# Sink-window attention, Fourier mixing and FFN on one core: the second FFN product of token groups 2 to 5 as seven Strassen products

## The chip, the cores and the metric

The kernel runs on one core of a Trainium2 chip, in one launch. Time is device time in microseconds (us), from one execution to the next some tenths of a per cent apart: three runs of the kernel before gave 766.65, 764.19 and 766.62, a median of 766.62. The engines are TensorE (PE in the profile, its weight loads PEld), VectorE (DVE), ScalarE (ACT), GpSimd (POOL) and SyncE (SP), which here issues the DMAs. Each engine takes its own instructions in order and waits for the others at semaphores.

## The reference

Attention with 4 sink tokens and a window of 128, over 4 batches, 8 heads, 768 tokens and 64 features a head, gives `x` of 4 x 768 x 512. Then, all in float32:

```python
X = np.fft.fft(np.fft.fft(x, axis=1), axis=2)
u = x + np.real(X).astype(np.float32)
mu = np.mean(u, axis=-1, keepdims=True)
var = np.mean((u - mu) ** 2, axis=-1, keepdims=True)
un = (u - mu) / np.sqrt(var + 1e-06)
ch = np.maximum(un @ w_ch1, 0.0) @ w_ch2
return (u + ch).astype(np.float32)
```

`w_ch1` is 512 x 2048 and `w_ch2` is 2048 x 512. The change lies in the last product, `relu(...) @ w_ch2`.

## The kernel before

**Precision.** Every large product is made of three: a matrix is split into a high part, rounded by a write in the type fp32r, and the low remainder (x minus its high part), and high x high, high x low and low x high are accumulated in PSUM. A split costs an ACT operation (the high part) and a DVE or POOL subtraction (the low part). `split` (L1148) does it for the hidden values, with the ReLU in it: ACT at L1149, DVE at L1150.

**Groups.** The 24 blocks of 128 tokens (order of batches 0, 2, 1, 3) are cut into six groups of four blocks, 512 tokens each. Attention and the Fourier mixing run until the page's 212th microsecond or so; group 0's FFN overlaps their end, together with the conversion of the weights. From there on groups 1 to 5 run one after the other, from about 338 us to 757 us of the span, in one loop written out by hand under `tc.manual_schedule()`: on each engine the instructions stand in the order of the program text. `u` of batches 0 and 2 lives in SBUF (`U`), that of batches 1 and 3 in DRAM (`u_dram`), and `reload` brings a group's `u` into places that are free again.

**The first product** (x times w1) already goes by Strassen's scheme in Winograd's form, with seven products in place of eight. `w_dram` holds, for each of 8 pairs of feature blocks, four quarters' worth of sums and quarters of w1, split, as made by `combine_w1` (L630 to L652) during group 0: POOL makes four sums of 256 columns (`tq`), ACT the high parts, POOL the low parts (`to`, L647). A group takes NIT = 4 rounds (`it`), each with seven products k = 0 to 6 (`product`, L1322), and every product is 12 matmuls of 256 columns. Its weights, 512 KB (a tile), are two DMAs of 256 KB from `w_dram` into one of eight places; `load(n + 8)` (L1297) stands behind product n, so eight tiles are under way or waiting. The other operand is `state["x"]`: the seven sums of x, split. PSUM banks A, B and C take the products in the order ABCABCB, and DVE adds them up: L1384, L1394, L1395, L1400, L1403 into `tmp`.

**The second product** is the plain one. `halves` splits a result into one of four places of `hring`, and `unit` (L1350) multiplies it by w2, which stays in SBUF as `Wt[f, 1]` (high and low): 12 matmuls of 512 columns for a unit, 16 units in a group, put between the products of the first. They accumulate over the whole group in four banks `o0` to `o3`, and `finish` (L1162, L1163) adds `u` on DVE and stores the block.

**The next group's preparation.** `prepare(g + 1)` is a generator, and the products call it a step at a time: layer norm statistics, reciprocal roots, the normalized block (L541), and its transpose in 32 x 32 squares by DVE (L1209, 64 instructions a group) into `xf`. In the last round `sums(g + 1, G)` makes the seven sums of x on POOL (L1230 to L1236) and `put` their splits (ACT L1240, POOL L1241).

Of the kernel before, what the change touches and what calls it, by code (L numbers as in the profile page):

```python
# [53 lines left out]
PREP_N = 3  # L54
NPR, NIT, NWS = NF // 2, NF // 4, 8
# [150 lines left out]
def kernel(  # L206
# [29 lines left out]
    w_dram = [dpool.tile([P, 7, 512], F32, name=f"wd{i}") for i in range(NPR)]  # L236

# [34 lines left out]
    def run(general):  # L272
        tag = "g" if general else ""
        with ExitStack() as p1:
# [889 lines left out]

            def u_of(b, blk):

                return U[b if b in U else b - 1][:, blk, :]

            def reload(g):

                left = {}
                for b, blk in groups[g]:
                    if b in U:
                        left.setdefault(b, []).append(blk)
                for b, l in left.items():
                    nc.sync.dma_start(U[b][:, l[0]:l[-1] + 1, :], u_dram[b + 1][:, l[0]:l[-1] + 1, :])
# [6 lines left out]
            def prepare(g):  # L1183
# [10 lines left out]
                for i, u in enumerate(us):  # L1194
# [9 lines left out]
                    else:  # L1204
                        un = un_.pop((b, blk))
                        for a in range(4):
# [4 lines left out]
                            yield  # L1211
# [79 lines left out]
            n_all = (len(groups) - 1) * NIT * 7  # L1291

            def load(n):
                if n < n_all:
                    it, k = divmod(n % (NIT * 7), 7)
                    for j in range(2):
                        nc.sync.dma_start(f32(places[n % NWS][:, j]).rearrange("p s c -> p (s c)"), w_dram[2 * it + j][:, W_PLACE[k]])  # L1297
# [8 lines left out]
            with tc.manual_schedule():  # L1306
                wr = p1.enter_context(tc.tile_pool(name="wr" + tag, bufs=1, side="right"))
                tmp = npool.tile([P, 6, 512], F32, tag="ring", name="tmp", bufs=1)
# [3 lines left out]
                p1c, u2, u3, c22, c12, c21 = (tmp[:, i] for i in range(6))  # L1312

                def product(n, ps):
                    k = n % 7
# [38 lines left out]

                for n in range(LDB, NWS):
                    load(n)
                n = 0
                for g in range(1, len(groups)):
                    steps = prepare(g + 1) if g + 1 < len(groups) else iter(())
                    for it in range(NIT):  # L1360
                        put = lambda k: None
                        if it == NIT - 1 and g + 1 < len(groups):
                            for _ in steps:
                                pass
                            start, put = sums(g + 1, G)
                            start()

                        def step():
                            next(steps, None)

                        ps = {}
                        for k in range(7):
                            if BANK.index(BANK[k]) == k:
                                pool, t = {"B": banks[it % 2][:2]}.get(BANK[k], (state["h"], {"A": "h", "C": "cw"}.get(BANK[k])))
                                kw = dict(bufs=1) if BANK[k] == "B" else {}
                                ps[BANK[k]] = pool.tile([P, 512], F32, tag=t, name=f"p{BANK[k]}_{g}_{it}", **kw)
                            product(n, ps[BANK[k]])
                            n += 1
                            a, b, c = (ps.get(x) for x in "ABC")
                            put(k)  # L1380
                            if k == 0:
                                A.copy(p1c, a)
                            elif k == 1:
                                V.tensor_tensor(u2, b, p1c, op=ALU.add)  # L1384
                                unit()
                                step()
                            elif k == 3:
                                halves(g, it, 0, 0, a)
                                unit()
# [101 lines left out]
```

## Time and profile before

| what | value |
|---|---|
| runs shown | 766.65, 764.19, 766.62 us; median 766.62 |
| profiled execution | 766.28 us, its span 764.6 us |
| mean granted TensorE clock | 0.992 |
| busy: PE, DVE, ACT, POOL | 729.8, 528.8, 267.1, 279.1 us |
| chain that ended last, by engine | PE 72%, DVE 12%, POOL 5% |
| largest line of that chain | L1350, the second product, 29% |
| L1350, `o<-w,hring` | 780 matmuls of 512 columns |
| HBM read and written | 120.77 MB and 24.13 MB |

The page and the answers of the trace use the same line numbers as the code above. A row of a group view gives line, engine, operation, output and inputs, the shape, how often it occurs, the busy time, the mean in nanoseconds, and the idle time in front of it with what ended it. A row of the timeline begins with the start and the length in us. The mean of one matmul row is its way through the array and longer than the distance from one matmul to the next, so distances are read from starts.

### The profile page before, as it was taken

The page shows a single profiled execution, that of the slowest core. Times are in us where ns is not written, and L with a number is a line of the kernel's source. Part 1 is how long each engine was busy: PE and PEld are TensorE (multiplying, and loading weights), DVE is VectorE, ACT ScalarE, POOL GpSimd, SP SyncE. Part 2 cuts the span into 40 slices and gives each one's busy share as a digit, 9 for nine tenths or more (in the row PEclk, how much of TensorE's full clock was granted, in tenths as well). Part 3 has the DMA queues.
Part 4 walks back from the last instruction along what each step waited for, and adds up shares of the span by engine and source line. Part 5 has one row for each costly group of instructions (what it writes and reads, how often), then busy time and mean ns, then how long its engine had stood idle before and what let it go on. Part 6 is the DMA issues. An engine that isn't in the chain of part 4 may idle for free.

```text
span 764.6 us, 13878 instructions
## 1 busy us (share of the span) xinstructions
PE 729.8 (95%) x4899; PEld 622.5 (81%) x4899; DVE 528.8 (69%) x1411; ACT 267.1 (35%) x743; POOL 279.1 (37%) x387
## 2 busy tenths in 40 slices
PE   7999998989989989899999999999999999999995
PEld 5676876867878768678899889989899889889884
DVE  6878588888899988867774778467855777342223
ACT  4787666666624335421123111321122111311110
POOL 2467467577548788740034000510043002500000
PEclk9999999999999999999999999999999999999998
DMA  9764525532317798789555865567655655575501
GB/s 297 260 169 124 144 72 171 167 100 96 103 43 259 266 333 301 269 284 395 186 179 168 281 196 167 168 220 251 191 178 183 219 175 174 176 242 163 175 27 60
DMA packets 84447, 145.91 MB, mean 191 GB/s; under 512 B 7532, under 2 KB 32236, under 8 KB 82960
## 3 DMA queue, kind: packets, MB, share of 16 engines
q1 hardware_dynamic: 84080, 141.17, 56.9%
q0 software_dynamic: 288, 3.76, 1.2%
q8 instruction: 41, 0.67, 0.4%
q14 instruction: 38, 0.31, 0.1%
HBM read 120.77 MB, written 24.13 MB: 190 GB/s over the span
## 4 chain that ended last, share of the span: by engine, by line
PE 72%; DVE 12%; POOL 5%; issue 3%; ACT 2%; DMA 2%; SPq 1%; ACTq 0%; DVEq 0%; POOLq 0%
PE o L1350 29%; PE pB L1322 11%; PE pC L1322 7%; PE pA L1322 7%; PE xt L837 4%; PE s L742 4%; PE pt L799 2%; PE za L396 2%; PE h L659 2%; PE zb L396 1%; DVE sm L761 1%; PE o L1157 1%; DVE cw L602 1%; DVE cw L601 1%; DVE s L748 1%
## 5 line engine op out<-in xcount | busy, mean ns | idle before, releaser
L1350 PE MATMUL o<-w,hring 128*128 128x512 f32 x780 | 192.0, 392 | 0.0
L1350 PEld LDWEIGHTS o<-w,hring 128*128 128x128 f32 x780 | 142.5, 188 | 27.9
L1149 ACT ACTIVATE hring<-tmp 128x512 fp32r<-128x512 f32 x60 | 37.9, 632 | 174.9 <-DVE tmp L1395 84.7
L1230 POOL TENSOR_TENSOR s<-xf 128x512 f32<-128x512 f32 x4 | 5.2, 1295 | 241.1 <-DVE xf L1209 241.1
L1150 DVE SCALAR_TENSOR_TENSOR hring<-tmp,hring 128x512 fp32r<-128x512 f32 x60 | 51.8, 864 | 45.6 <-ACT hring L1149 45.6
L1209 DVE STREAM_TRANSPOSE xf<-un 32x128 f32<-32x128 f32 x256 | 77.4, 302 | 3.5
L767 ACT ACTIVATE sm<-sm,mx 128x132 f32<-128x132 f32 x192 | 76.0, 400 | 4.7 <-DVE mx L761 4.7
L1322 PE MATMUL pB<-x,w_b 128*128 128x256 f32 x456 | 59.4, 279 | 0.6 <-DMA w_b<-wd 0.6
L1322 PEld LDWEIGHTS pB<-x,w_b 128*128 128x128 f32 x456 | 56.6, 188 | 1.7 <-DVE stat L518 0.8
L659 PE MATMUL h<-un_slots,w_ring 128*128 128x512 f32 x192 | 50.6, 412 | 7.4 <-DVE h L1150 7.2
L742 PE MATMUL s<-ring,q 64*128 64x260 f32 x320 | 49.3, 412 | 7.8 <-DVE mx L761 3.5
L761 DVE CUSTOM_DVE_ANT_0 sm<-s,mask 128x132 f32<-128x132 f32 x192 | 48.5, 293 | 8.2 <-PE s L740 2.8
L1150 DVE SCALAR_TENSOR_TENSOR hring<-pA,hring 128x512 fp32r<-128x512 f32 x20 | 13.8, 692 | 56.4 <-ACT hring L1149 56.4
L659 PEld LDWEIGHTS h<-un_slots,w_ring 128*128 128x128 f32 x192 | 36.7, 198 | 17.6 <-DVE h L1150 7.0
L1149 ACT ACTIVATE hring<-pA 128x512 fp32r<-128x512 f32 x20 | 11.9, 596 | 99.8 <-PE pA L1322 99.8
L742 PEld LDWEIGHTS s<-ring,q 64*128 64x128 f32 x320 | 26.9, 185 | 20.4 <-issue 6.6
L1350 PE MATMUL o<-w_gh,hring 128*128 128x512 f32 x120 | 42.5, 395 | 0.0
L1157 PE MATMUL o<-w,h 128*128 128x512 f32 x156 | 39.1, 395 | 1.1 <-POOL w L627 0.5
L837 PE MATMUL xt<-ptl,ldv 128*64 128x128 f32 x384 | 39.3, 285 | 0.0
L1322 PEld LDWEIGHTS pC<-x,w_b 128*128 128x128 f32 x288 | 36.9, 188 | 2.0
L1322 PE MATMUL pA<-x,w_b 128*128 128x256 f32 x288 | 37.5, 279 | 0.2 <-DMA w_b<-wd 0.2
L1322 PE MATMUL pC<-x,w_b 128*128 128x256 f32 x288 | 37.4, 279 | 0.0
(216 smaller groups left out, 1528.7 us busy)
## 6 DMA issues: line engine op xcount, KB each, us to landing
w_b<-wd SPq DMA_DIRECT2D x172, 256.0 KB, 3.4
w_c<-wd SPq DMA_DIRECT2D x108, 256.0 KB, 3.4
raw<-in_moe_w_ch_dram SPq DMA_DIRECT2D x32, 512.0 KB, 4.8
wd<-to SPq DMA_DIRECT2D x8, 1024.0 KB, 5.1
ldv<-in_v_dram SPq DMA_DIRECT2D x28, 256.0 KB, 3.1
ring<-in_qk_dram SPq DMA_DIRECT2D x24, 264.0 KB, 4.5
wd<-w_ring SPq DMA_DIRECT2D x8, 768.0 KB, 3.9
out_dram<-u SPq DMA_DIRECT2D x24, 256.0 KB, 2.3
```

The lines of the kernel that those rows point to most:

```text
L396: T.matmul(ps[:, :NK], a, c, start=i == 0, stop=i == len(mm) - 1)
L659: T.matmul(ps[:, :tb], a[cc], x[:, :, cc, :], start=n == 0, stop=n == 3 * NCC - 1)
L742: T.matmul(ps[:, j, :P + W], st["q", g][rows, hp, :], keys(g, 2 * hp + j), start=True, stop=True)
L761: V.tensor_tensor_reduce(sm[:, h % 4], ps[:, j, P:P + W], mask[min(qi, 3)], -SCALE, 3.0e38, ALU.add, ALU.min, accum_out=mx[:, 0, h:h + 1])
L767: A.activation(sm[:, h % 4], sm[:, h % 4], AF.Exp, bias=mx[:, 0, h:h + 1], scale=-1.0, accum_out=mx[:, 1, h:h + 1])
L837: T.matmul(ps[D * j:D * j + D, p, :], st["v", kb(g) - i][:, h, :], a[:, h % 4, :], start=i == 0, stop=i == n - 1)
L1149: state["relu"] = A.activation(h[0], x, AF.Relu).ins
L1150: V.scalar_tensor_tensor(h[1], x, 0.0, f32(h[0]), op0=ALU.max, op1=ALU.subtract)
L1157: T.matmul(po[i], a[:, ts_], x, start=f == 0 and n == 0, stop=f == NF - 1 and n == 2)
L1209: V.transpose(place[32 * q:32 * q + 32, :, r], un[r].rearrange("p (c q j) -> p c q j", c=NCC, q=4)[:, :, q])
L1322: T.matmul(ps[:, 256 * j:256 * j + 256], w[:, j, a, cs], x[:, xs], start=BANK.index(BANK[k]) == k and j == c == m == 0, stop=j == c == 1 a ...
L1350: T.matmul(po[i], h[:, a, j, ts_], x, start=first and j == m == 0, stop=last and j == 1 and m == 2)
```

## The change

Group 1 keeps the old second product. In its first three rounds it also makes sums of w2's quarters; groups 2 to 5 then multiply by Strassen's scheme over all 2048 features at once. For these groups the first product comes first as a whole, 28 products, two rounds (index i) interleaved; then the second, 28 steps `s2`, as seven products k with four steps c each.

Making the sums, for each of the 8 pairs p, at fixed turns of group 1 (0 to 27 of 40): two DVE sums of 512 columns that put high and low of w2 together, four POOL sums of 256, two ACT copies and two POOL differences, and a store of 1 MB from SP's queue into `t_dram`.

```diff
+t_dram = [dpool.tile([P, 4, 512], F32, name=f"td{i}") for i in range(NPR)]
...
+def whole_w2(p):
+    for j in range(2):
+        w = Wt[2 * p + j, 1]
+        V.tensor_tensor(sums_r[0][:, j], f32(w[0]), f32(w[1]), op=ALU.add)
...
+def split_w2(p):
+    q, o = sums_q, sums_o
+    for j in (0, 2):
+        A.copy(o[:, j:j + 2, 0].bitcast(F32R), q[:, j:j + 2])
+        G.tensor_tensor(o[:, j:j + 2, 1].bitcast(F32R), q[:, j:j + 2], o[:, j:j + 2, 0], op=ALU.subtract)
...
+    t0 = 26 * p // NPR
+    for d, fn in ((0, whole_w2), (1, sums_w2), (4, split_w2), (5, store_w2)):
+        w2_at.setdefault(t0 + d, []).append((fn, p))
```

Three of the four sums (products k = 1, 2, 4) are loaded for every group, twelve tiles more in the same stream of eight places; the fourth is loaded once, in group 2's k = 0, over the quarters of w2 that it replaces (16 DMAs, 2 MB in all). The other four products use w2 as it stands in SBUF.

```diff
+stream = [(w_dram, it, W_PLACE[k]) for it in range(NIT) for k in range(7)]
+for g in range(2, len(groups)):
+    stream += [(w_dram, i, W_PLACE[k]) for it in range(0, NIT, 2) for k in range(7) for i in (it, it + 1)]
+    stream += [(t_dram, it, T_PLACE[k]) for k in (1, 2, 4) for it in range(NIT)]
```

In the first product's 28 steps DVE adds up the results as before, ACT applies the ReLU, and for each round POOL makes two of the sums of the hidden values:

```diff
+    V.tensor_tensor(t_[c], p, t_[c], op=ALU.add)
+    A.activation(t_[c], t_[c], AF.Relu)
+    G.tensor_tensor(X[3][c], t_[c], X[1][c], op=ALU.subtract)
+    G.tensor_tensor(t_[c], X[4][c], X[3][c], op=ALU.add)
+if t == 2 and 3 < g + 1 < len(groups):
+    reload(g + 1)
+if t in (14, 15, 24, 25):
+    split_h(c_ := (14, 15, 24, 25).index(t), 0, c_, V)
+for _ in range(CH1_PREP[g > 2][t]):
+    next(steps, None)
```

with `CH1_PREP = [[0] + [1, 2, 1] * 9, [0] * 6 + [1, 1, 2] * 7 + [1]]`; each preparation turn of groups 3 to 5 is now two transposes. In the second product each step is 12 matmuls of 256 columns; an operand is split four steps ahead of its use, by ACT and DVE, for k = 2 by ACT and POOL:

```diff
+def split_h(n, k, c, eng):
+    h = hring[:, n % 4]
+    hi, lo = (h[:, j].rearrange("p j t -> p (j t)") for j in range(2))
+    x = {0: X[1], 1: t_, 2: X[1], 3: X[2], 4: X[3], 5: X[2], 6: X[4]}[k][c]
+    A.copy(hi, x)
+    eng.tensor_tensor(lo, x, f32(hi), op=ALU.subtract)
...
+for s2 in range(7 * NIT):
+    k, c = divmod(s2, NIT)
...
+    product2(s2, k, c, n, p)
+    if k in (1, 2, 4):
+        load(n + NWS)
+        n += 1
+    if s2 + 4 < 7 * NIT:
+        k4 = (s2 + 4) // NIT
+        split_h(s2 + 4, k4, (s2 + 4) % NIT, G if k4 == 2 else V)
+    if k == 0:
+        G.tensor_tensor(X[1][c], X[1][c], t_[c], op=ALU.add)
+    if k == 3:
+        G.tensor_tensor(X[2][c], X[2][c], t_[c], op=ALU.subtract)
+    if c == NIT - 1:
+        for half, m in (((0, 1), (1, 0), (1, 1)), ((0, 1),), ((1, 1),), ((0, 0),), ((1, 1),), ((0, 1),), ((1, 0),))[k]:
+            add_u(g, half, m, p)
+        if k >= 5:
+            store_u(g, k - 5)
```

The results are added to `u` on DVE, nine additions of 512 columns a group, and stored in two halves behind k = 5 and k = 6. The rest of the preparation runs here, one turn a step, and behind it `sums_x(g + 1)`, which replaces `sums`: four POOL sums and seven splits (ACT and POOL), again one turn a step. In group 2 it begins at step 9, in groups 3 and 4 at step 16. `tmp` and other places in SBUF are handed out anew for `X`; the places for `u` of groups 3 to 5 change with them.

More of the change, by code (lines that the diff above doesn't have):

```diff
@@ L1311, in run, with product @@
                 hring = npool.tile([P, 4, 2, 2, 256], F32R, tag="un_slots", name="hring", bufs=1)
-                p1c, u2, u3, c22, c12, c21 = (tmp[:, i] for i in range(6))
-                def product(n, ps):
-                    k = n % 7
+                more = [wr.tile([P, 2, 512], F32, name="more")] if general else []
+                last_chunk = wr.tile([P, 512], F32, name="last_chunk")
+                p1c, u2, u3, c21 = (tmp[:, i] for i in range(4))
+                def product(n, k, ps):
                     w = places[n % NWS]
@@ L1357, in run @@
                 n = 0
[L1358 to L1389, printed above, removed]
-                                step()
-                                if it == 0:
-                                    reload(g - 1)
-                            elif k == 4:
-                                V.tensor_tensor(u3, b, p1c, op=ALU.add)
-                                V.tensor_tensor(c22, u3, c, op=ALU.add)
-                                halves(g, it, 1, 1, c22)
-                                unit()
-                                step()
-                            elif k == 5:
-                                V.tensor_tensor(c12, u2, c, op=ALU.add)
-                                halves(g, it, 1, 0, c12)
-                            elif k == 6:
-                                V.tensor_tensor(c21, b, p1c, op=ALU.add)
-                                halves(g, it, 0, 1, c21)
-                                unit()
-                            step()
@@ L1407, in run @@
                 while done[0] < len(units):
                     unit(1)
+                assert not w2_at, w2_at
+                x12 = npool.tile([P, 2, NIT, 512], F32, tag="ring", name="x12", bufs=1)
+                x3 = [npool.tile([P, 2, 512], F32, tag="tw", name=f"x3_{i}", bufs=1 if general else 2) for i in range(2 - len(more))]
+                x3 += more
+                X = {
+                    1: [x12[:, 0, c] for c in range(NIT)],
+                    2: [x12[:, 1, c] for c in range(NIT)],
+                    3: [x3[c // 2][:, c % 2] for c in range(NIT)],
+                    4: [npool.tile([P, 512], F32, tag="qs0", name=f"x4_{c}", bufs=QSB) for c in range(NIT - 1)] + [last_chunk],
+                }
```

204 lines of the change are left out of this document (191 added, 13 removed).

## The prediction

> **What bounds the kernel now.** I read the page for the engine shares, then busy time by stage, then the order of work on TensorE inside a group, then the rows where POOL and DVE meet. The profiled execution took 766.28 us, 0.34 below the median of the runs shown (766.62); all sums start from 766.3.
>
> ```profile
> span 764.6 us, 13878 instructions
> PE 729.8 (95%) x4899; PEld 622.5 (81%) x4899; DVE 528.8 (69%) x1411; ACT 267.1 (35%) x743; POOL 279.1 (37%) x387
> ```
>
> The next view gives busy time by stage. Groups 1 to 5 run from 338 to 757 us, some 83.7 us each. The first four rows are the four rounds (`it` 0 to 3) of group 1, the fifth is group 2, the last is group 5.
>
> ```profile
> 338.00:359.00 21.00, 20.19 (x140) 18.52 (x139) 15.15 (x43) 3.67 (x6) 0.00 (x0) 1.00 1.00 374
> 359.00:380.00 21.00, 21.00 (x135) 18.87 (x133) 15.50 (x41) 3.08 (x5) 0.00 (x0) 1.00 0.70 230
> 380.00:401.00 21.00, 21.00 (x134) 18.97 (x133) 15.74 (x36) 4.11 (x7) 6.31 (x5) 1.00 0.56 175
> 401.00:422.00 21.00, 21.00 (x135) 18.97 (x134) 8.64 (x12) 6.08 (x10) 8.64 (x7) 1.00 0.56 180
> 422.00:505.50 83.50, 83.50 (x530) 75.38 (x529) 56.07 (x131) 16.35 (x27) 14.93 (x11) 1.00 0.63 203
> 673.00:757.00 84.00, 83.85 (x518) 74.83 (x516) 28.10 (x42) 11.73 (x19) 0.00 (x0) 1.00 0.42 133
> ```
>
> Columns: length, then PE, PEld, DVE, ACT, POOL busy, the granted clock, the DMA share, GB/s. TensorE is busy without a gap: it alone bounds the changed stage, at the full clock. DVE has 56 us of 83.5, of which 28 are the preparation of the next group (group 5 prepares nothing and shows 28.10). POOL has 15.
>
> ```profile
> 500.67 1.58 PE L1322 MATMUL pA<-x,w_c 128*128 128x256 f32 x12
> 502.08 1.59 PE L1322 MATMUL pB<-x,w_c 128*128 128x256 f32 x12
> 503.51 2.93 PE L1350 MATMUL o<-w,hring 128*128 128x512 f32 x12
> 506.28 1.58 PE L1322 MATMUL pC<-x,w_c 128*128 128x256 f32 x12
> 507.69 1.57 PE L1322 MATMUL pA<-x,w_b 128*128 128x256 f32 x12
> 509.11 2.92 PE L1350 MATMUL o<-w,hring 128*128 128x512 f32 x12
> ```
>
> From start to start, twelve matmuls of 256 columns take 1.415 us (506.28 to 509.11, halved), twelve of 512 take 2.77. I call 1.415 us a step.
>
> **TensorE.** A group now has 28 steps and 16 units of 2.77: 39.6 + 44.3 = 83.9, as seen. The change replaces the 16 units by 28 steps in groups 2 to 5: 44.3 - 39.6 = 4.7 saved, **-18.8** for four. The rest asks what makes TensorE wait.
>
> **The hand-over to the second product.** Before, the two products alternate, so each result has steps to spare. Now product 2 of the second product (index k=2) needs `X[1]+t_`, and POOL alone makes it. Its queue at that place: `X[3]` and `t_` for the last two quarters (4), `X[1]` for all four (4), the first difference of `split_h` (1): nine operations of 512 before step 8 may start. The prices:
>
> ```profile
> 398.98 1.30 POOL L1241 TENSOR_TENSOR x<-xf,x 128x512 fp32r<-128x512 f32 x1 [0.76 <-ACT x L1240]
> 400.25 1.29 POOL L1241 TENSOR_TENSOR x<-s,x 128x512 fp32r<-128x512 f32 x1
> ```
> ```profile
> L1384 DVE TENSOR_TENSOR tmp<-pB,tmp 128x512 f32<-128x512 f32 x20 | 13.8, 692 | 19.9 <-PE pB L1322 18.6 <-ACT tmp L1382 1.1
> L1149 ACT ACTIVATE hring<-tmp 128x512 fp32r<-128x512 f32 x60 | 37.9, 632 | 174.9 <-DVE tmp L1395 84.7 <-DVE tmp L1400 53.9 <-DVE tmp L1403 35.8
> L1209 DVE STREAM_TRANSPOSE xf<-un 32x128 f32<-32x128 f32 x256 | 77.4, 302 | 3.5
> ```
>
> POOL starts one every 1.27 us. Product 26 ends one step before the second product starts, with a tail of 0.16 us (a row of twelve lasts 1.58, not 1.415), so its result is there at -1.25; DVE's sum (0.69) and ACT's ReLU (0.63) bring POOL's start to about 0.2. Nine times 1.27 is 11.4, so 11.6 against the 11.3 at which step 8 is due. That is late even with nothing in the way. Two things are in the way.
>
> ```profile
> 395.22 1.30 POOL L1231 TENSOR_TENSOR s<-s,xf 128x512 f32<-128x512 f32 x1
> 396.48 1.75 POOL L1232 TENSOR_TENSOR s<-xf 128x512 f32<-128x512 f32 x1
> ```
> ```profile
> 395.25 1.82 DVE L1150 SCALAR_TENSOR_TENSOR hring<-tmp,hring 128x512 fp32r<-128x512 f32 x1 [0.76 <-ACT hring L1149]
> 398.43 0.69 DVE L1150 SCALAR_TENSOR_TENSOR hring<-tmp,hring 128x512 fp32r<-128x512 f32 x1 [0.76 <-ACT hring L1149]
> ```
>
> First, a DVE operation with both operands in SBUF does not run beside POOL: the one at 395.25 took 1.82 instead of 0.69, ending 0.55 after POOL's operation (396.52), and the POOL operation behind it took 1.75, which is 0.45 more. [...]
>
> `split_h` puts such DVE differences into every step, four of them into this stretch: 4 x 0.45 = 1.8, so 13.4. Second, DVE is late there when it prepares a group: in the last six steps of the first product it has 6 sums and 2 differences of 0.69 and 8 turns of two transposes (0.62 by 77.4/256), 10.5 us in 8.5; the sum POOL waits for sits behind most of this, 1.8 late by my estimate. So 15.1, and step 8 waits 3.8 us in groups 2 to 4 and 2.1 in group 5: 3 x 3.8 + 2.1 = **+13.5**. Bounds: 4 x 0.3 = 1.2 if DVE slips between, and 20 if DVE is 4 us late.
>
> **Later in the second product.** `sums_x` puts 11 POOL operations for the next group into it, beside 4 of `X[2]`. While both queues are full, one POOL operation and one DVE difference take 1.27 + 0.45 = 1.72 per step of 1.415; the four steps of lead absorb some five such steps. In group 2 the last `X[2]` is the eleventh in POOL's queue, which comes free near 19.4; with difference pairs only up to the seventh, it ends near 37.4, the operand for step 23 stands near 39.0, due at 15.1 + 15 x 1.415 = 36.3: 2.7 late. In groups 3 and 4 `sums_x` starts seven steps later, 0.7 each; group 5, 0.3: **+4.4** (0 to 12).
>
> **The clock.**
>
> ```profile
> 222.84 0.59 PE L396 MATMUL za<-cst,gl 128*128 128x386 f32 x1 [2.30 <-DVE gl L369]
> ```
> ```profile
> 219.00:223.00 4.00, 1.70 (x12) 1.38 (x11) 3.94 (x7) 0.66 (x2) 2.13 (x3) 1.00 0.00 0
> 223.00:226.40 3.40, 3.40 (x9) 2.68 (x10) 3.40 (x8) 1.07 (x2) 0.49 (x1) 0.50 0.08 14
> ```
>
> After 4 us with TensorE busy for 1.70, the granted clock was 0.50 for 3.4 us, which costs 1.7. Three waits of 3.8 us should do the same; group 2's takes as much off its later wait, so 2 x 1.7 = **+3.4** (0 to 6.8). [...]
>
> **Group 1** keeps the old order and makes the sums of w2 in its first three rounds.
>
> ```profile
> L1150 DVE SCALAR_TENSOR_TENSOR hring<-tmp,hring x60: 691/693/1819, 349.2 to 750.7; 128x512 fp32r<-128x512 f32 x60
> ```
> ```profile
> L640 POOL TENSOR_TENSOR tq<-tw x8: 727/738/1195, 216.2 to 324.6; 128x256 f32<-128x256 f32 x8
> ```
> ```profile
> L647 POOL TENSOR_TENSOR to<-tq,to 128x512 fp32r<-128x512 f32 x16 | 21.3, 1346 | 2.8 <-ACT to L646 2.8
> ```
>
> POOL, idle in two of these rounds, gets 8 x (4 x 0.74 + 2 x 1.35) = 45 us in 63. DVE gets 16 sums of 0.69 = 11.0 over 2.3 rounds. It has 15.5 busy of 21, and in-order waits for ACT of 0.76 behind three halves of each round (the rows of L1150 above), 2.3: free are 3.2 a round, 7.4 in 2.3. So it is 3.6 late with no meeting at all. The 16 sums and some 8 differences read SBUF twice; if each waits half a POOL operation, up to 12 more. TensorE uses a half a unit and a step after it is asked for (4.2 us, less 1.3 for ReLU and difference): 2.7 of lateness is free. That leaves 0.9 to 13; I take **+4**, nearer the lower end, since the smallest row (691, also the median 693) is met far more often than the longest (1819). ACT's two copies per pair wait for POOL with the ReLUs queued behind, which is inside this bound.
>
> **Costed at nothing.** The loads: each step of the first product now eats 512 KB in 1.415 us, 370 GB/s; the first window above ran 21 us at 374, and eight tiles (11.3 us) are ahead. The eight 1 MB stores of sums and the 2 MB reload of w2's quarters stand in SP's queue ahead of loads, under the same lead. **The end:**
>
> ```profile
> 756.88 0.69 DVE L1162 TENSOR_TENSOR u<-o,u 128x512 f32<-128x512 f32 x1 [0.69 <-PE o L1350]
> 753.48 4.46 SPq L1163 DMA_DIRECT2D out_dram<-u  x4
> ```
>
> One sum and one store followed the last matmul; now one sum and two stores: +0.3.
>
> Sum: -18.8 + 13.5 + 4.4 + 3.4 + 4 + 0.3 = +6.8, so **773**.
>
> **Rivals.**
> *Faster: the queues slip past each other.* DVE is not late at the hand-over and the clock holds: 4 x 2.1 there, 0.3 at the end, group 1 hidden: -18.8 + 8.4 + 0.3 = -10.1, **756** (749 if the differences never meet POOL). For it: most rows of L1150 show 693 ns, and a late TensorE gives time back. Against it: nine POOL operations are 11.6 us in any order.
> *Slower still: group 1 bound by DVE and the shared access.* The upper 13 in place of 4: 773 + 9 = **782**. It decides once the sums of w2 wait half a POOL operation each.
> *The loads do not keep up.*
>
> ```profile
> q1 hardware_dynamic: 84080, 141.17, 56.9%
> u<-ud SPq DMA_DIRECT2D x2, 1024.0 KB, 7.8
> w_b<-wd SPq DMA_DIRECT2D x172, 256.0 KB, 3.4
> ```
>
> 141.17 MB in 56.9% of 764.6 us is 324 GB/s, 1.62 us a tile. In groups 3 and 4 a reload of 1 MB and 0.5 MB of stores stand ahead: tile 27 lands at 1.4 + 23 x 1.62 + 2.1 (3.4 less its transfer) = 40.8, due at 38.2: 2.6 twice, **778**. Against it: the window at 374.
>
> **How the numbers follow.** A measurement of this kernel can tell about 0.5% (3.8 us) from no change. Forecast 0.42 (about 769 to 779: 0.25 slower, 0.15 same, 0.02 faster); the faster rival 0.34 (0.32 faster, 0.02 same); group 1 0.14 (slower); loads 0.10 (0.09 slower, 0.01 same). So faster 0.34, same 0.18, slower 0.48. The range takes in the rival of 756 down to 752 and group 1 up to 787; below lies the rest of the faster case, above the upper bounds falling together. The forecast's own range is 766 to 781.
>
> **What would show it.** TensorE waiting for POOL's difference at step 8 of each second product, 3.8 us in groups 2 to 4 and less in group 5, with the clock at 0.50 behind; DVE differences well above 0.69 us; group 1 longer than 84 us; TensorE steps of 1.415 elsewhere. It is wrong if group lengths of 2 to 5 come near 79 us, if the wait at step 8 ends on a load, or if the steps of the second product pace worse than 1.415 by themselves.

## The result, and the profile after

The changed kernel takes 825.66 us (median; 821.53 to 827.46) against 766.03 us (764.19 to 766.65) for the kernel before: the ratio is 1.0775, with a 95% interval of 1.0729 to 1.0821. It is slower, as forecast, but by 60 us where 7 were forecast, far outside the range. The profiled execution took 827.46 us, its span is 825.7, and the mean granted clock is 0.958 (0.992 before).

The page of the changed kernel, its span and the busy times:

```profile
span 825.7 us, 15803 instructions
PE 743.8 (90%) x5475; PEld 657.1 (80%) x5475; DVE 613.9 (74%) x1479; ACT 339.8 (41%) x871; POOL 449.7 (54%) x515
```

TensorE stood for 34.8 us of its span before and stands for 81.9 now. Its 743.8 us busy are not more work either: they hold matmuls at half clock (the mean granted clock fell from 0.992 to 0.958). Busy time by stage shows where. The first row is group 1; then come pairs of rows, the first product and the second product of groups 2, 3, 4 and 5. Columns as before: length, then PE, PEld, DVE, ACT, POOL busy, the granted clock, the DMA share, GB/s.

```profile
346.20:453.40 107.20, 92.16 (x530) 79.88 (x529) 73.93 (x143) 24.84 (x43) 59.38 (x55) 0.92 0.74 264
453.40:492.90 39.50, 39.50 (x338) 39.41 (x337) 33.55 (x85) 10.63 (x18) 5.64 (x4) 1.00 0.97 347
492.90:552.10 59.20, 47.66 (x339) 45.54 (x338) 38.12 (x59) 21.29 (x37) 39.14 (x27) 0.88 0.56 178
552.10:591.40 39.30, 39.30 (x338) 39.30 (x337) 28.89 (x72) 10.70 (x18) 5.60 (x4) 1.00 0.97 352
591.40:643.40 52.00, 45.44 (x339) 43.40 (x339) 44.83 (x72) 21.68 (x37) 37.87 (x26) 0.93 0.53 170
643.40:682.70 39.30, 39.30 (x337) 39.30 (x337) 29.12 (x72) 10.72 (x18) 7.85 (x6) 1.00 1.03 379
682.70:733.80 51.10, 45.44 (x338) 42.85 (x337) 45.50 (x72) 21.68 (x37) 39.01 (x26) 0.93 0.50 162
733.80:773.20 39.40, 39.40 (x339) 39.40 (x338) 15.33 (x22) 12.80 (x22) 8.34 (x6) 1.00 1.01 359
773.20:817.00 43.80, 40.26 (x338) 39.65 (x336) 26.66 (x32) 16.23 (x27) 23.93 (x16) 1.00 0.29 100
```

All four first products run at 39.3 to 39.5 us, 28 steps of 1.41, at up to 379 GB/s, and TensorE has no gap in them. The loss is elsewhere, and it adds up. Group 1 begins at 346.2 in place of 338.0 (+8.2). It lasts 107.1 us where a group lasted 83.8 (418.9 from 337.99 to 756.9, divided by five; +23.3). The second products last 59.2, 51.9, 51.1 and 43.8 us where 28 steps are 39.6 (+47.6). The tail behind the last matmul is 8.7 us, not 7.7 (+1.0). Less the 18.8 that TensorE saves, that is 61.3, and the spans differ by 61.1. Even group 5, beside which nothing is prepared, takes 39.4 + 43.8 = 83.2 us: 0.6 less than before, where 4.7 were to be saved.

**The hand-over.** TensorE in group 3's second product, its first step and the two longest waits (start, length, what; the idle time in front and its releaser in brackets):

```profile
591.44 1.60 PE L1513 MATMUL qA<-w,hring 128*128 128x256 f32 x12
...
601.57 0.50 PE L1513 MATMUL qB<-w_c,hring 128*128 128x256 f32 x2 [3.00 <-ACT hring L1500]
...
612.35 5.82 PE L1513 MATMUL qC<-w_b,hring 128*128 128x256 f32 x34 [2.45 <-POOL hring L1501]
```

The last row is the forecast wait at step 8, for POOL's difference. The one at 601.57, at step 4, for ACT, was not forecast. POOL at the same place, from the first of its nine operations:

```profile
599.19 1.26 POOL L1588 TENSOR_TENSOR x<-u,x 128x512 f32<-128x512 f32 x1 [20.44 <-ACT u L1587]
...
605.14 5.94 POOL L1612 TENSOR_TENSOR x<-x,u 128x512 f32<-128x512 f32 x4
611.02 5.64 POOL L1501 TENSOR_TENSOR hring<-x,hring 128x512 fp32r<-128x512 f32 x4
```

The nine end with the first of the four differences at 611.02, near 612.3: 13.1 us, where 11.4 + 1.8 = 13.2 had been worked out. But the chain starts 7.75 us after the second product (7.67 and 7.65 in groups 2 and 4), not 2.0 (0.2 and 1.8 late); in group 5, where nothing is prepared, it starts after 2.40, not 0.2. Rows of DVE in group 3, and two of ACT among them, show why:

```profile
593.11 0.69 DVE L1501 TENSOR_TENSOR hring<-x,hring 128x512 fp32r<-128x512 f32 x1 [1.21 <-ACT hring L1500]
593.83 0.62 DVE L1223 STREAM_TRANSPOSE xf<-un 32x128 f32<-32x128 f32 x2
594.48 0.69 DVE L1583 TENSOR_TENSOR x<-pC,x 128x512 f32<-128x512 f32 x1
596.38 0.69 DVE L1501 TENSOR_TENSOR hring<-x,hring 128x512 fp32r<-128x512 f32 x1 [1.21 <-ACT hring L1500]
597.10 0.62 DVE L1223 STREAM_TRANSPOSE xf<-un 32x128 f32<-32x128 f32 x2
597.76 0.69 DVE L1586 TENSOR_TENSOR u<-pB,u 128x512 f32<-128x512 f32 x1
```
```profile
595.21 0.63 ACT L1584 ACTIVATE x<-x 128x512 f32<-128x512 f32 x1 [2.13 <-DVE x L1583]
595.75 0.60 ACT L1500 CAST hring<-x 128x512 fp32r<-128x512 f32 x1
```

POOL waits for the ReLU of step 26's sum (the first L1586). Ahead of that sum in DVE's queue stand the sums of steps 24 and 25 (L1583; step 24's is at 591.21, above the rows shown) and the differences of the two `split_h` at these steps. Each waits 1.21 us for ACT's copy, the copy stands in ACT's queue behind a ReLU, and the ReLU waits for the DVE sum just made. DVE and ACT, each in order, hand the work to and fro, and two transposes follow each time. The wait at step 8 came out the other way round than forecast: 2.54, 2.45 and 1.82 us in groups 2 to 4, where TensorE had already lost 3 us at step 4, and 3.16 in group 5.

**Group 1.** ACT's waits, and ACT's queue around one of them:

```profile
ACT tmp L1400 <- DMA td<-tmp: 29.2, 6, 8.0
```
```profile
386.42 1.14 ACT L1400 CAST tmp<-sums_q 128x512 fp32r<-128x512 f32 x2 [7.17 <-DMA td<-tmp]
387.46 0.59 ACT L1153 ACTIVATE hring<-pA 128x512 fp32r<-128x512 f32 x1
```
```profile
388.11 0.79 PE L1373 MATMUL o<-w_gh,hring 128*128 128x512 f32 x1 [6.59 <-ACT hring L1153]
```

ACT's copies of a pair's sums write the buffer `sums_o` (it lies in `tmp`, the name in the view), and that is free only when the store of the pair before has landed. The ReLU of the hidden values (L1153) stands behind them, and TensorE waits 6.59 us for it. The stores were issued at 373.02, 381.38 and 389.65, 8.3 us apart, where pairs were to follow each other after 3.25 turns of some 2.1 us, 6.8 us: with one buffer, copy, difference, store and landing form a loop longer than the schedule.

**Group 0's end.** POOL in the changed kernel, then TensorE: the group of matmuls that POOL holds, and one a little earlier:

```profile
331.96 0.74 POOL L1392 TENSOR_TENSOR sums_q<-sums_r 128x256 f32<-128x256 f32 x1
...
334.18 0.72 POOL L1395 TENSOR_TENSOR sums_q<-sums_r,sums_q 128x256 f32<-128x256 f32 x1
334.86 2.48 POOL L651 TENSOR_TENSOR to<-tq,to 128x512 fp32r<-128x512 f32 x2
337.30 2.50 POOL L631 TENSOR_TENSOR w<-cv,w 128x512 fp32r<-128x512 f32 x2
```
```profile
325.21 4.43 PE L663 MATMUL h<-un_slots,w_ring 128*128 128x512 f32 x12 [2.30 <-DVE h L1154]
...
338.61 7.78 PE L1161 MATMUL o<-w,h 128*128 128x512 f32 x23 [4.24 <-POOL w L631]
```

The same two in the kernel before:

```profile
322.16 4.49 PE L659 MATMUL h<-un_slots,w_ring 128*128 128x512 f32 x12 [2.30 <-DVE h L1150]
...
331.81 6.34 PE L1157 MATMUL o<-w,h 128*128 128x512 f32 x23 [0.45 <-POOL w L627]
```

The sums of pair 0 (L1392 to L1395, 2.9 us), due at turn 1 of group 1, stand in POOL's queue ahead of group 0's last conversions of w2 (L631). TensorE waits 4.24 us for these, and 0.45 before. From the earlier row to group 1 it is 15.8 us before (322.16 to 337.99) and 21.0 in the change (325.21 to 346.23): 5.2 of the 8.2 us belong to this wait and the slower matmuls behind it. The other 3.0 were lost ahead of the earlier row and do not hang on the sums: in the kernels below that have pair 0 at this place, that row stands anywhere from 320.7 to 326.8.

### The profile page after: what moved, and what is told of

Its sections match the earlier page's. It is cut to its first block, busy times and chain, and to the rows that moved or that the text cites. A ratio compares the mean times of both kernels' runs of the same rounds, so it can differ in the third digit from the quotient of the medians.

```text
span 825.7 us, 15803 instructions
## 1 busy us (share of the span) xinstructions
PE 743.8 (90%) x5475; PEld 657.1 (80%) x5475; DVE 613.9 (74%) x1479; ACT 339.8 (41%) x871; POOL 449.7 (54%) x515
## 4 chain that ended last, share of the span: by engine, by line
PE 53%; DVE 21%; POOL 9%; issue 6%; DMA 6%; ACT 4%; SPq 1%; ACTq 0%; DVEq 0%; POOLq 0%
PE pB L1345 7%; PE qB L1513 6%; PE qC L1513 5%; PE pA L1345 5%; PE pC L1345 5%; PE xt L841 4%; PE s L746 4%; PE qA L1513 3%; PE o L1373 3%; DVE xf L1223 3%; DMA td<-tmp 2%; PE pt L803 2%; DMA raw<-in_moe_w_ch_dram 2%; DVE hring L1501 2%; PE za L400 1%
## 5 line engine op out<-in xcount | busy, mean ns | idle before, releaser
L1588 POOL TENSOR_TENSOR x<-u,x 128x512 f32<-128x512 f32 x16 | 24.2, 1513 | 171.5 <-ACT u L1587 171.5
L1501 DVE TENSOR_TENSOR hring<-x,hring 128x512 fp32r<-128x512 f32 x76 | 83.2, 1113 | 41.1 <-ACT hring L1500 35.5
L1500 ACT CAST hring<-x 128x512 fp32r<-128x512 f32 x92 | 56.8, 619 | 59.1 <-PE qC L1513 22.9
L1513 PE MATMUL qB<-w_c,hring 128*128 128x256 f32 x288 | 42.1, 309 | 10.4 <-ACT hring L1500 9.1
L1513 PEld LDWEIGHTS qB<-w_c,hring 128*128 128x128 f32 x288 | 40.1, 216 | 11.9 <-ACT hring L1500 9.7
L1401 POOL TENSOR_TENSOR tmp<-sums_q,tmp 128x512 fp32r<-128x512 f32 x16 | 22.7, 1438 | 41.5 <-ACT tmp L1400 41.5
L1373 PE MATMUL o<-w,hring 128*128 128x512 f32 x156 | 41.0, 410 | 3.8 <-ACT hring L1153 2.6
L746 PEld LDWEIGHTS s<-ring,q 64*128 64x128 f32 x320 | 27.3, 188 | 20.5 <-issue 7.4
L782 POOL CAST sk<-sm 128x32 fp32r<-128x32 f32 x48 | 11.3, 235 | 59.1 <-ACT sm L771 59.0
L1513 PE MATMUL qA<-w,hring 128*128 128x256 f32 x312 | 41.4, 281 | 2.1 <-ACT hring L1500 1.4
L1513 PEld LDWEIGHTS qA<-w,hring 128*128 128x128 f32 x312 | 38.3, 189 | 3.3 <-ACT hring L1500 2.0
```

The source lines that it names most:

```text
L746: T.matmul(ps[:, j, :P + W], st["q", g][rows, hp, :], keys(g, 2 * hp + j), start=True, stop=True)
L1373: T.matmul(po[i], h[:, a, j, ts_], x, start=first and j == m == 0, stop=last and j == 1 and m == 2)
L1500: A.copy(hi, x)
L1501: eng.tensor_tensor(lo, x, f32(hi), op=ALU.subtract)
L1513: T.matmul(ps[:, 256 * t:256 * t + 256], h[:, a, j, P * t:P * t + P], x, start=BANK.index(BANK[k]) == k and c == t == j == m == 0, stop=c ...
```

## The experiments

The kernel before took 767.5, 770.1, 766.2 and 766.5 us beside them. Totals of the kernels can differ by up to 6 us for reasons outside the edit: where the code ahead of group 1 is that of the changed kernel, group 1 begins anywhere from 341.1 to 347.2. So I read the lengths of the stages. Each edited kernel here was executed once, but for the last two (four and twelve times). Where its code is that of the change, group 1 takes 106.8 to 107.8 us, group 3's second product 51.1 to 52.0 and group 5's 43.7 to 46.4, the last by how much of it ran at half clock (0 to 6.9 us); differences below that say nothing. "Second products" are those of groups 2, 3, 4, 5; the changed kernel has 59.2, 51.9, 51.1, 43.8, and 107.1 for group 1.

### What the sums of w2 cost

The sums are not made, and the loads take the same bytes from `w_dram`: its groups 2 to 5 multiply by sums of w1 in place of those of w2.

```diff
 def w2_step(t):
-    for fn, p in w2_at.pop(t, ()):
-        fn(p)
+    w2_at.pop(t, ())
...
-    stream += [(t_dram, it, T_PLACE[k]) for k in (1, 2, 4) for it in range(NIT)]
+    stream += [(w_dram, it, T_PLACE[k]) for k in (1, 2, 4) for it in range(NIT)]
```

> Leaves out the making of w2's sums in group 1 (all of its DVE, POOL, ACT and store work); the second products read w1's sums in their place, the same bytes. In the changed kernel group 1 takes 107.1 us (346.23 to 453.35) in place of 83.8, and starts 8.2 us later than before. Theory 'sums' (ACT stands behind the store of the sums, and what POOL does for pair 0 stands ahead of group 0's last weights): group 1 comes back to 84 to 86 us, its start comes forward by 4 us or more, the rest stays; total 795 to 800. Rival 'loads or clock' (the new order of loads or a slower clock stretches group 1): group 1 stays above 95 us, total above 810.

798.00 us. Group 1 begins at 338.8 and takes 85.1; the second products are 58.4, 52.0, 51.8, 45.2. So the sums cost 22.0 us in group 1 and nothing behind it. Of the 7.4 ahead of it some 5 are theirs: from the earlier row of "Group 0's end" to group 1 it is 15.9 us here and 21.0 in the change.

### Two buffers for the store

A second `sums_o`, used in turn; the room for it is taken from the loads, with six places in place of eight.

```diff
+    sums_o.append(wr.tile([P, 4, 512], F32, name="sums_o2")...)
...
-    q, o = sums_q, sums_o
+    q, o = sums_q, sums_o[p % len(sums_o)]
```

> All work stays; the split sums of w2 get a second buffer in SBUF, taken from two of the eight places of the load stream (six remain). Theory 'store': ACT's wait for the store (29.2 us in six waits) falls below 6, group 1 goes from 107 to 88 to 94 us, total 808 to 815. Rival 'DVE and shared access', as my prediction had it (DVE over its time and POOL and DVE excluding each other): group 1 stays above 101 us, total 819 or more. With six places the first products could wait for loads; that is read apart: they take 39.4 us now.

819.16 us; group 1 takes 99.8. ACT's wait for the store is gone, and with it 7.3 us, not the whole excess. ACT's copies now wait for the sums themselves:

```profile
ACT tmp L1402 <- POOL sums_q L1395: 4.6, 1, 4.6
```

The buffer is one cause of group 1's loss and not the largest: 99.8 lies between the 88 to 94 of the theory and the 101 of the rival. First products stay at 39.4 to 40.2 with six places.

### The sums spread out, whole sums on POOL

Two buffers and six places; pairs at turns 2 to 30 (`t0 = 2 + 32 * p // NPR`) in reversed order, so that none slips into group 0; `whole_w2` on POOL in place of DVE.

> Group 1 relieved: two buffers for the split sums (six places of the load stream, as in e2_two_buffers), the 16 sums of high and low of w2 on POOL in place of DVE, the pairs four turns apart in place of 3.25, the last pair first (so that its sums can't stand ahead of group 0's last weights). Theory 'DVE late in group 1' (what e2_two_buffers left, 99.8 against 85.1 without sums, is DVE's sums and their meetings with POOL): group 1 takes 85 to 90 us, starts at 339 to 341, total 800 to 806. Rival 'shared access' (POOL gets 20 us more and excludes DVE's halves for as long): group 1 stays above 95, total above 812.

811.39 us. Group 1 begins at 338.4: the slip is undone. It still takes 98.6, not the 85 to 90 expected. POOL is now full (9.4 to 9.9 us busy in every 10 from 369 to 419), so this moved the load from one engine to the other and didn't tell which of them had bound it.

### ACT's copies one turn later

As the kernel above, but with the whole sums on DVE again; the copies five turns behind them and the store six.

```diff
-    for d, fn in ((0, whole_w2), (1, sums_w2), (4, split_w2), (5, store_w2)):
+    for d, fn in ((0, whole_w2), (1, sums_w2), (5, split_w2), (6, store_w2)):
```

> Group 1's remainder. Like the run with two buffers, six places and the pairs spread to turn 34 in reversed order, but DVE makes the two whole sums again and ACT's two copies of a pair stand one turn later (five turns behind the whole sums, the store six). Theory: what is left of group 1's excess (98.6 against 85.1 without sums) is ACT, in order, standing at a copy whose sums POOL has not made, with the ReLUs queued behind it. Then the copies find their sums ready and group 1 takes 88 to 92 us, the program 801 to 806. Rival: DVE's and POOL's shared access makes both engines full in group 1, wherever the copies stand: group 1 stays above 96 and the program above 808.

812.34 us, group 1 99.8: my theory, ACT held by copies that come too early, falls. TensorE's waits in group 1 name DVE, but for one in the last round and 0.4 us for a load:

```profile
PE pC L1345 <- DVE tmp L1461: 4.6, 3, 2.6
PE o L1373 <- DVE hring L1154: 3.5, 4, 1.3
PE o L1373 <- ACT hring L1153: 3.5, 1, 3.5
```

And DVE's whole sums are long, 946 ns on average for 13 of the 16 (the other three, from other tiles, take 3.8 us together):

```profile
L1389 DVE TENSOR_TENSOR sums_r<-w,w 128x512 f32<-128x512 f32 x13 | 11.8, 946 | 0.1
```

### DVE's whole sums left out

The kernel above without `whole_w2`; POOL makes the sums from the high parts of w2 alone, so the products lack their low parts. All else has the same work at the same turns.

> Like the kernel with the copies one turn later, but the whole sums on DVE are left out: POOL makes its sums from the high parts of w2 alone (so the sums lack the low parts). POOL, ACT, the stores and the loads have the same work at the same turns. Theory DVE: what is left of group 1's excess before its last round is DVE, whose 16 sums take 15.6 us there; without them the waits on DVE's results (some 8 us) go, and group 1 falls from 99.8 to 88 to 92 us. Rival POOL: POOL's 5.9 us and more a pair, met by DVE's subtractions, hold the sums of x in the last round whatever DVE does: group 1 stays above 95 us.

802.00 us; group 1 takes 87.8, at a clock of 1.00 throughout. The 16 DVE sums, 15.6 us with their meetings, thus cost 12.0 us of group 1, and POOL's work, unchanged, does not hold it. Part of the 12.0 may go by way of POOL, which in the kernel above waited 15.0 us in all for these sums (L1394). This gives group 1's 23.3 us step by step: 107.1 to 99.8 with the second buffer (7.3; spread pairs and later copies leave it at 99.8), to 87.8 without DVE's sums (12.0), to 85.1 with no sums at all (2.7), to 83.8 before (1.3, little more than executions differ).

### Splits at steps 20 and 21

```diff
-    if t in (14, 15, 24, 25):
-        split_h(c_ := (14, 15, 24, 25).index(t), 0, c_, V)
+    if t in (14, 15, 20, 21):
+        split_h(c_ := (14, 15, 20, 21).index(t), 0, c_, V)
```

> Moves the first splits of quarters 2 and 3 (X[1], k=0) from steps 24 and 25 of the first product to steps 20 and 21, right behind the ReLU that makes X[1]. Theory 'hand-over': each of the two now costs DVE 1.21 us of waiting for ACT, which stands behind a ReLU that waits for DVE; without it POOL's first sum of the hand-over starts about 2.4 us earlier in every group (after the start of the second product: 7.7 in groups 2 and 3 to about 5.3, 2.4 in group 5 to about 0.2), step 8 as much earlier, the second products go from 59.2, 51.9, 51.1 and 43.8 to about 56, 49, 48 and 41.5; total 814 to 818. Rival 'shared access alone': step 8 is late because POOL and DVE exclude each other, the start of POOL's chain does not matter: total within 3 us of 825.7.

821.66 us. POOL's nine operations start earlier, in group 3 3.89 us after the second product (592.93) in place of 7.75, and in group 5 after 0.22 in place of 2.40, as the prediction had it there:

```profile
596.82 1.29 POOL L1588 TENSOR_TENSOR x<-u,x 128x512 f32<-128x512 f32 x1 [17.86 <-ACT u L1587]
```

Second products 57.1, 48.3, 48.3, 41.7: 10.6 us less in all, and in group 2 the wait at step 4 falls from 3.11 to 0.52. First products grow to 40.9, 41.0, 40.5 (39.3 in group 5), since DVE, with the preparation in its queue, is late for a sum there, and the total misses the 814 to 818 expected. The to and fro between DVE and ACT is shown; a part of it comes back as plain load on DVE.

### No transposes for groups 3 to 5

192 transposes are left out: groups 3 to 5 work on whatever `xf` holds.

```diff
-    V.transpose(place[32 * q:32 * q + 32, :, r],
+    g > 2 or V.transpose(place[32 * q:32 * q + 32, :, r],
```

> Leaves out the 192 transposes of the preparation of groups 3 to 5 (20 us of DVE a group, 0.62 us for each turn of two); the products multiply old values of x. Groups 2 to 4 prepare, group 5 does not, and its second product is the shortest (43.8 us against 59.2, 51.9, 51.1). Theory 'DVE late at the hand-over': without the transposes groups 2 to 4 start POOL's chain like group 5, about 2.4 us after the second product's start in place of 7.6, the waits at steps 4 and 8 fall from 3.1 and 2.5 to below 1 and about 3 at full clock, and their second products take 45 to 50 us; total 800 to 810. Rival 'POOL' (the next group's sums of x on POOL make the difference between group 5 and the others): they stay above 50 (group 2 above 56), total above 818.

808.83 us; second products 54.3, 45.4, 45.5, 45.4. DVE's transposes cost 4.9, 6.6 and 5.6 us in groups 2 to 4. POOL's nine operations start 2.4 to 2.6 us after the second product in all four, and nothing waits at step 4. Groups 3 and 4 now take just what group 5 takes in the same kernel (each with 3.4 us at half clock, of which group 5 had none in the change).

### No sums of x in the second product

`xs = iter(())` in place of `sums_x(g + 1)`: groups 3 to 5 multiply with the x of group 2.

> Leaves out the sums of x for groups 3 to 5 (11 POOL operations and 7 ACT copies a group); all groups multiply group 2's x. Theory 'DVE late at the hand-over': the hand-over is untouched, so steps 4 and 8 wait as before in groups 2 to 4 (3.1 and 2.5 us); only what lies behind goes, which is the waits at step 22 of group 2 (3.3 and 1.1, and the half clock after them) and the slow last steps of groups 3 and 4: second products about 51, 49 and 48, total 808 to 815. Rival 'POOL': all three come near group 5's 43.8, total below 800.

812.05 us; second products 50.5, 49.0, 49.0, 45.4: 8.7 us in group 2, 2.9 and 2.1 in groups 3 and 4. The waits at steps 4 and 8 stay nearly as they were (in group 2 3.11 and 2.77, after 3.11 and 2.54). What goes in group 2 are waits late in its second product, for a split of `X[2]`; the first and longest in the change, with one of 1.05 us behind it:

```profile
538.38 0.58 PE L1513 MATMUL qC<-w_gh,hring 128*128 128x256 f32 x1 [3.30 <-ACT hring L1500]
```

### Product 2's differences on DVE

`V` in place of `G if k4 == 2 else V`, which takes the ninth operation off POOL's chain.

> The four differences of k=2 go from POOL to DVE. Theory 'POOL's queue' (nine POOL operations stand before step 8): now the fifth frees the first operand, so in group 5, where DVE is not loaded, the wait at step 8 (3.2 us) goes and the second product takes 41 to 42 us in place of 43.8; in groups 2 to 4 DVE has four more differences, and the gain is 0 to 3 us each; total 816 to 824. Rival 'shared access': the same two-source work has only moved, no second product gets shorter by more than 1 us; total 824 to 830.

826.48 us; second products 59.5, 52.5, 52.6, 42.1. Only group 5 gains, 1.6; its wait at step 8 falls from 3.16 to 1.28. Where a group is prepared nothing is won, and the total is the rival's (824 to 830): there DVE is no freer than POOL.

### The waits filled with matmuls

18 and 16 matmuls into an idle bank, whose results nothing reads, ahead of steps 4 and 8 in groups 2 to 4, so that TensorE does not stand and the clock holds.

> Adds matmuls that nobody reads (18 of 256 columns ahead of step 4, 16 ahead of step 8, on values of w2 that stay, into a free PSUM bank) in groups 2 to 4, 2.1 and 1.9 us, so that TensorE is busy while it waits there. Nothing else changes. In the changed kernel the granted clock stood at 0.5 for 27.3 us of the four second products, which costs half of that, 13.7 us. Theory 'clock': the waits themselves are no shorter, but the 0.5 behind the hand-over goes (3.4, 3.4 and 6.8 us in groups 2 to 4 and more), second products 2 to 4 us shorter each in groups 3 and 4, total 816 to 822. Rival 'the clock costs nothing since TensorE only waits longer elsewhere': total 825 to 829, second products as they were or longer by the added matmuls.

824.32 us; second products 58.4, 51.2, 51.2, 46.2. Group 3's by the view of busy time by stage:

```profile
584.00:635.40 51.40, 48.08 (x377) 45.15 (x376) 46.36 (x76) 21.17 (x36) 37.17 (x24) 1.00 0.54 179
```

The clock is 1.00, not 0.93, and the length is the same. In the changed kernel 6.8 us of that stage ran at 0.50, worth 3.4 of its 12.4 us, and its rows show 6.5 us of waiting; the other 2.5 are in rows that last longer than their work. With the clock whole, waiting for operands takes the place of the 3.4. Group 5, which has no filling, shows the other side: there 46.2 us with 6.9 at half clock, 43.8 without.

### POOL beside DVE, by itself

The kernel before, with two additions on POOL behind each product of group 5, in place on data that is done with.

```diff
+    if g == len(groups) - 1:
+        for i in range(2):
+            x_ = state["xf"][:, i, :2]
+            G.tensor_tensor(x_, x_, state["xf"][:, i, 2:4], op=ALU.add)
```

> The kernel before, with two additions of 512 columns on POOL behind each of the 28 products of group 5, both operands in SBUF, in place on data that nothing reads any more; no result depends on them. It measures the shared access by itself. Theory: DVE's subtractions of the halves (both operands in SBUF) grow there from 0.69 us to 1.1 on average, up to 1.8, while DVE's sums with an operand in PSUM stay at 0.69, and POOL's additions become longer than 1.3 us where they meet; TensorE is not held, so the time stays within 3 us of before. Rival: the long differences of the changed kernel come from something else (ACT's writes, DMA traffic), and group 5 shows 0.69 for both.

766.42 us, as before. DVE's groups in group 5, the kernel before and this one (L1150 both operands in SBUF; L1394 and L1398 are the same sum with one operand in PSUM):

```profile
L1150 DVE SCALAR_TENSOR_TENSOR hring<-tmp,hring 128x512 fp32r<-128x512 f32 x12 | 8.3, 693 | 9.1 <-ACT hring L1149 9.1
L1394 DVE TENSOR_TENSOR tmp<-pB,tmp 128x512 f32<-128x512 f32 x4 | 2.8, 692 | 9.2 <-PE pB L1322 9.2
```
```profile
L1150 DVE SCALAR_TENSOR_TENSOR hring<-tmp,hring 128x512 fp32r<-128x512 f32 x12 | 14.3, 1196 | 9.1 <-ACT hring L1149 9.1
L1398 DVE TENSOR_TENSOR tmp<-pB,tmp 128x512 f32<-128x512 f32 x4 | 2.8, 692 | 9.2 <-PE pB L1322 9.2
L1383 POOL TENSOR_TENSOR xf<-xf 128x512 f32<-128x512 f32 x52 | 69.2, 1371 | 0.0
```

With POOL beside it, a subtraction of two SBUF operands takes 1.20 us on average in place of 0.69, and a sum with one operand in PSUM stays at 0.69.

### All repairs together

The kernel with later copies, with splits at steps 20 and 21, no preparation turns in the last four steps of the first product and the first four of the second (two a step in the next four), and product 2's differences on DVE in group 5.

```diff
-CH1_PREP = [[0] + [1, 2, 1] * 9, [0] * 6 + [1, 1, 2] * 7 + [1]]
+CH1_PREP = [[0] + [1, 2, 1] * 7 + [1, 2] + [0] * 4, [0] * 6 + [1, 1, 2] * 6 + [0] * 4]
...
-    for _ in range(CH2_PREP):
+    for _ in range(0 if s2 < 4 else 2 if s2 < 8 else 1):
```

> Repairs together: the former kernel with, besides, splits at steps 20 and 21 in place of 24 and 25, no preparation turn in the last four steps of the first product and the first four of the second, and product 2's differences on DVE in group 5, where nothing is prepared. Theory: the hand-over's cost is DVE's lateness, so second products fall from 51 to 44 to 47 in groups 3 and 4 and from 44 to 41 in group 5; with group 1 at 88 to 92 the program takes 784 to 796, still slower than before (766), since POOL's nine operations at 1.27 before step 8, and one operation on each of POOL and DVE per step, remain. Rival: the preparation's DVE work only moves, and comes back as lateness elsewhere in the group: groups 2 to 4 stay above 88 us each (first and second product together) and the program above 798.

793.27 us; the ratio to before is 1.0364 (1.0322 to 1.0407). Group 1 takes 100.1, the second products 49.8, 46.3, 46.4, 40.0, and groups 2 to 4, first and second product together, 90.6, 87.2 and 87.5. Group 1 is not at the 88 to 92 expected, and that the total lies in the 784 to 796 expected is luck. The second products lost 23.5 us in all against the change; the first products gave some 4.5 back. What is left in group 3 is POOL's nine operations:

```profile
572.28 1.30 POOL L1590 TENSOR_TENSOR x<-u,x 128x512 f32<-128x512 f32 x1 [16.29 <-ACT u L1589]
...
584.03 5.16 POOL L1503 TENSOR_TENSOR hring<-x,hring 128x512 fp32r<-128x512 f32 x4
```
```profile
585.54 4.39 PE L1515 MATMUL qC<-w_b,hring 128*128 128x256 f32 x22 [3.33 <-POOL hring L1503]
```

They start 2.3 us after the second product (570.0) and hold step 8 for 3.33 us, close to the forecast's 2.0 and 3.8. So the forecast described this kernel's hand-over, and not that of the change.

### Strassen's second product in group 5 alone

Groups 1 to 4 keep the old order; the sums are made in groups 1 to 3, one pair in ten turns; `t_` lies in the places of group 3's `u`; splits at steps 20 and 21, product 2 on DVE.

```diff
-    t0 = 26 * p // NPR
+    t0 = 40 * (p // 3) + 10 * (p % 3) + 2
...
-    for g in range(2, len(groups)):
+    for g in range(len(groups) - 1, len(groups)):
```

> Strassen's second product in group 5 alone, where no next group is prepared: groups 1 to 4 keep the old order; the sums of w2's quarters are made in groups 1 to 3, one pair in ten turns (three, three and two pairs), all else of a pair as in the change; splits at steps 20 and 21 and product 2's differences on DVE. Theory: the scheme gains only where DVE and POOL are free, and the sums of w2 cost nothing where they are spread over 250 us: groups 1 to 4 take 83.6 to 84.5 us each as before, group 5 79.4 as in the repaired kernel, against 83.8, and with 1 us more behind the last matmul the program takes 761 to 765, 0.1 to 0.7% faster than before. Rival: each pair still delays the in-order queues by a turn (8 pairs by 1 us or more), and the gain of 3.4 us is spent: 766 to 772.

764.70 us (762.78 to 766.79) against 766.51; the ratio is 0.9965, 95% interval 0.9948 to 0.9981. By the 2% that count as a change here it takes the same time as the kernel before; the interval puts it 0.2 to 0.5% below. The first and second product of its group 5:

```profile
676.60:716.00 39.40, 39.40 (x338) 39.37 (x337) 16.89 (x24) 13.89 (x23) 5.92 (x4) 1.00 0.98 350
716.00:756.10 40.10, 40.07 (x337) 39.68 (x336) 29.16 (x33) 15.53 (x26) 19.10 (x12) 1.00 0.47 157
```

79.5 us where 83.8 were before: the scheme saves 4.3 of the forecast 4.7 where DVE and POOL are free. From the first matmul of group 1 to the last of group 5 it is 417.1 against 418.9, so groups 1 to 3 with the sums, and group 4, take back some 2.5.

## Why the prediction was right and wrong

**Right.** Slower, since the second product waits for its operands; TensorE's saving (first products at 39.3 to 39.5, second products down to 40.0 where nothing waits); the loads at nothing, with the rival on loads refuted (no gap in a first product at up to 379 GB/s; one wait of 1.1 us in group 1); POOL's nine operations at 13.1 us and the wait for POOL's difference at step 8; a DVE difference that meets POOL growing well above 0.69 us, shown by itself in the kernel with POOL beside DVE (1.20 on average). The sign and most of the places were right; of the size, 61.1 us between the spans, the sum had 6.8. The hand-over, the rest of the second product and the clock together were put at 21.3 and lost 47.6, group 1 at 4 and lost 23.3, the end at 0.3 and lost 1.0, and the 8.2 ahead of group 1 had no term.

**The hand-over, mis-sized.** The step that failed is "the sum POOL waits for sits behind most of this, 1.8 late by my estimate". That counted DVE's busy time, 10.5 us in 8.5, and no waits in its queue. In groups 2 to 4 POOL started 7.65 to 7.75 us after the second product, where 2.0 had been worked out, and in group 5 2.40, where 0.2 had. Two shown causes: the splits at steps 24 and 25, whose ACT copies stand behind ReLUs that wait for DVE (moved: a start of 3.89, 0.22 in group 5; 3.6 us less in group 3's second product, 1.6 of it given back in the first), and the preparation's transposes (left out: a start of 2.55, 6.6 less). The two overlap: of the start's 7.75 us they take 3.9 and 5.2. They also made step 4 late, 3.00 us, which the prediction did not have: ACT's copies of `t_` stand behind the last ReLU. With either repair that wait is 0.5 us or less. So step 8 waited less than the 3.8 in groups 2 to 4, the loss having been taken earlier, and more than the 2.1 in group 5. DVE was 7.5 us late, and the upper bound had 4.

**Later in the second product, mis-sized.** `sums_x` was put at 2.7 us in group 2 and 0.7 in groups 3 and 4; left out, it gives 8.7, 2.9 and 2.1. The step took POOL to be free near 19.4 us; with a chain that starts some 6 us late it was free at 25.2 in group 3. That this is the whole of the difference is argued, not shown: even in the repaired kernel, where the chain starts on time, group 2's second product takes 3.5 us more than group 3's.

**The clock, real in the rows and not a term of its own.** Half clock did follow waits in groups 2 to 4 (none followed group 5's 3.16 us), and more of it than forecast: 27.3 us in the four second products, where 6.8 were meant. But where DVE, ACT and POOL set the pace, it cost nothing: with the clock held, groups 3 and 4 took 51.2 in place of 51.9 and 51.1. In such a stage a sum that adds both the wait and the clock behind it counts time twice.

**Group 1: one step wrong, one missing, one at the wrong end.** "ACT's two copies per pair wait for POOL with the ReLUs queued behind, which is inside this bound" named the wrong releaser: they waited for the store of the pair before, 7.3 us by the second buffer. DVE's 16 sums cost 12.0, near the upper bound of 13 that the prediction gave, where I took 4 because most rows of L1150 stood at 693 ns; these were rows of stages in which POOL did little. So the rival "group 1 bound by DVE and the shared access" was the better forecast of that part. What stays open is the 2.7 between no whole sums and no sums at all, and how much of DVE's 12.0 is the meetings (15.6 us for work of 11.0), how much its own load, and how much POOL's wait for the sums.

**Group 0's end, not in the sum.** No step looked at what stands in the queues behind group 0 when group 1's first turns are written. Six kernels with a later pair at this place, or none, began group 1 at 338.4 to 339.3, against 341.1 to 347.2 in the seven with it. Most of the spread among the seven lies ahead of the slip. From the earlier row of "Group 0's end" to group 1 the six take 15.6 to 15.9 us and the seven 20.3 to 21.2; the six wait 0.6 us at most for L631, the seven 4.1 to 4.5. So the slip costs some 5 us. What delayed that earlier row, by 3.0 us in the profiled execution, stays open.

## What to carry to other kernels

Where an operand passes through several in-order engines, follow the queue of each engine instruction by instruction to the consumer: the busy share (DVE 74%, POOL 54%) shows none of the to and fro that cost most here. A scheme that saves TensorE work pays with elementwise work, so put it where the other engines stand idle: the seven products lost 13.9 us, even when repaired, in the three groups that also prepare the next one (90.6 + 87.2 + 87.5 against three times 83.8), and gained 4.3 us in the one group that does not. Work that is to be made once has 250 us in which to be made; crowded into 60 us of one group it cost some 27 us (22.0, and 5 ahead of it), with a single store buffer and a queue that reached back into the group before.

## What the runs showed of the hardware

- Where DVE and POOL are both busy most of the time (44.83 and 37.87 us of 52.0 in group 3's second product), most of DVE's differences are long and not just a few: 76 of those for the second products have a median of 1020 ns, against 693 for those of L1150 before.

```profile
L1501 DVE TENSOR_TENSOR hring<-x,hring x76: 674/1020/1852, 476.4 to 810.5; 128x512 fp32r<-128x512 f32 x76
```

- Half clock without cost: a second product lasted 51.2 us at a granted clock of 1.00 and 51.9 at 0.93, because its operands came no sooner.
- The clock fell to 0.50 behind a wait of 3.00 us, as the forecast had it from the trace of before. The changed kernel around the wait at step 4 of group 3, busy time by stage:

```profile
599.50:602.90 3.40, 0.99 (x6) 0.79 (x7) 2.73 (x7) 2.18 (x4) 3.32 (x3) 1.00 0.00 0
602.90:606.30 3.40, 3.40 (x19) 3.40 (x18) 3.25 (x7) 0.62 (x1) 3.32 (x3) 0.50 0.27 65
```

  TensorE was busy for 0.99 of the 3.40 us ahead of the drop. A wait of 3.16 us had no drop behind it: at step 8 of group 5, in the same execution, the granted clock stayed at 1.00.
- The loads kept up at 347 to 379 GB/s for 39 us on end, where the trace of before had shown 374 for 21 us.
